# First chunk's attention of a fused attention and two-MLP kernel: two pairs of units with their own buffers in a hand-set order, and W1, W2 decoded 1024 wide

## The chip, the cores and the metric

The kernel runs on one core of one Trainium2 chip. The metric is the device time of one execution in microseconds. Three runs of the kernel before took 773.91, 776.0 and 777.68 us, median 776.0.

## The reference

Three stages follow each other on 4 sequences of 576 positions, model width 512 (8 heads of 64):

```python
# 1. attention, per head: two softmaxes, added
q_d, k_d, v_d = (mean of 4 neighbouring positions of q, k, v)     # 144 rows
out_up = repeat(softmax(scale * q_d @ k_d.T) @ v_d, 4)
out_local = softmax(where(|i - j| < 4, scale * q @ k.T, -1e9)) @ v
x = out_up + out_local                                            # -> (4, 576, 512)
# 2. first MLP, a residual around it
xn = (x - mean(x)) / sqrt(var(x) + 1e-6) * g_ln
x = x + relu(xn @ w_ch1) @ w_ch2                                  # 512 -> 2048 -> 512
# 3. second MLP with a shift by one position
xk = mu_k * x + (1 - mu_k) * x_prev;  xr = mu_r * x + (1 - mu_r) * x_prev
out = sigmoid(xr @ w_r) * (relu(xk @ w_k) ** 2 @ w_v)             # 512 -> 1024 -> 512
```

The weights come in float64. The activations are float32.

## The kernel before

The 2304 positions are cut into six chunks of 384 (`N`). A chunk's attention is four *units*, one per pair of heads (`unit(c, hp, nxt)`). A unit sums q over four positions (line 354, `prep`), sums k (line 357 in chunk 0, by accumulating DMAs later), makes the dense scores of the summed rows (`scd`, line 419) and the windowed scores in 32-column tiles (`sc`, line 423), does the two softmaxes on DVE and ACT (lines 429 to 463), turns the probabilities around (line 477 on DVE for the windowed ones, line 493 on PE for the dense ones, copies at 481 and 496), multiplies by v (`av`, lines 506 and 515) and adds both into `x` (line 524). [...] The first MLP takes its 16 blocks of 128 hidden features in turn (`emit_l1`, `emit_l2`): twelve products (four k-blocks, three products each: high by high, high by low, low by high) give one block of the first layer in `h_ps`, and twelve more add it into the four output banks `acc`.

W1 and W2 arrive as float64, are decoded to float32 and split in two on the chip, piece by piece (`conv_gen`, `decode`). A piece is 128 rows by 512 numbers. It takes three steps on ACT (line 84: the high word, scaled; line 89: the three bits below; line 93: the rounded high part) and three on DVE (line 85: the sign; line 90: shift and or; line 96: the remainder, the low part). The generator does half a piece at each call, and overlaps the last steps of one piece with the first steps of the next. `pieces_w12` gives the order: four pieces of W1, three of W2, and so on, so that a block of W1 comes just ahead of the hidden features that need it. `ensure(key)` runs the generator until a piece is finished; it stands ahead of the products that read the piece.

The order of work is laid down in two ways. The instructions carry dependencies, and a scheduler orders each engine's queue by program order and readiness; `in_order(True, ins)` pins an instruction behind everything that was written for its engine before. In the program text, small generators are advanced in turns: the opening (lines 768 on) issues the first loads in the order of the string `ORDER`, then feeds one `Attn` object with a budget of `PROB` = 800 per turn; it opens a unit when the one before has reached its softmax, so that units overlap by about half; from the tenth turn on the weight generator is called in three of ten turns. When the attention of chunk 0 is over, the first MLP of chunk 0 starts, and `slot(c)` between its products feeds chunk 1's attention and calls the weight generator once (line 803 on). The pinned fillers `idle` (line 375, eight products of 128 columns ahead of each product step) and `warm` (line 365, 512 columns) do no useful work.

Chunk 0's value sums are additions on POOL (lines 345, 346). All loads go out on SP's queue; the accumulating sums for later chunks go out on POOL's queue (lines 324, 325).

Of the kernel before, what the change touches and what calls it, by code (L numbers as in the profile page):

```python
# [8 lines left out]
F32 = mybir.dt.float32  # L9
# [12 lines left out]
SD = S // 4  # L22
# [16 lines left out]
def tile_block(ctx: ExitStack, tc: tile.TileContext, qw, kw, kf, kr, vw, vr, vec, mask, w1, w2, wk, wv, wr, out):  # L39
# [16 lines left out]
    ident = const.tile([2 * QB, 2 * QB], F32, name="ident")  # L56
# [50 lines left out]
    def pieces_w12():  # L107
        for p in range(4):
            yield from (("w1", p, k) for k in range(KT))
            yield from (("w2", f // 4, f % 4) for f in range(max(4 * p - 1, 0), 4 * p + 3 if p < 3 else NF))  # L110

    def conv_gen():
        keys = list(pieces_w12())
        late_keys = [k for k in keys if k[:2] == ("w2", 3)]
        raws, todo = {}, iter([k for k in keys if k not in late_keys])

        def fetch():
            key = next(todo, None)
            while key in raws:
                key = next(todo, None)  # L120
            if key is None:
                return
            nm, p, k = key
            src = w1s[:, :, 1024 * p:1024 * p + 1024] if nm == "w1" else w2s[:, 4 * p:4 * p + 4, :]
            t = wpool.tile([128, 2, 1024], I32, tag="w", name="raw")
            for i in range(2):
                raws[nm, p, k + i] = t[:, i]
            for i in range(2):
                in_order(len(raws) < 9, nc.sync.dma_start(t[:, i], src[:, k + i]))

        def fetch_late(key):
            if key in late_keys:
                t = stg.tile([128, 1024], I32, tag="stg", name="raw", bufs=RB)
                nc.sync.dma_start(t, w2s[:, 12 + key[2], :])
                raws[key] = t
# [7 lines left out]
        for n, key in enumerate(keys + [None]):  # L143
# [3 lines left out]
            if key:  # L147
                nm, p, k = key
# [4 lines left out]
                w1st = next(g)  # L153
# [3 lines left out]
            if last:  # L157
                in_order(pin, split_lo(h, l, w))
                done.add(last)
            if key:  # L160
                h, l, w = W[p][0][:, k, :], W[p][1][:, k, :], w1st
            last = key
            if n % 2 == 1 or n > 24 or n == 4:
                fetch()
# [123 lines left out]
    qds, chains, firsts, raw_k, means = {}, [], [], {}, {}  # L288
# [5 lines left out]
    Ps = [pone.tile([128, 2 * NG, 32], F32, name=f"P{i}") for i in range(2)]  # L294
# [38 lines left out]
    def first_k(hp):  # L333

        if not firsts:
            firsts.append(pln.tile([128, KT, N], F32, tag="xc", name="kf").rearrange("p k n -> p (k n)"))
        t = firsts[0][:, S * (hp % 2):S * (hp % 2) + S]
        in_order(True, nc.sync.dma_start(t, kf[0, hp]))
        kd, _ = sum_tiles(0, hp)
        raw_k[hp] = kd, t  # L340

    def first_v(hp):
        t = xp.tile([128, KT, N], F32, tag=("ah", "al")[hp % 2], name="vr", bufs=1).rearrange("p k n -> p (k n)")[0:KD, 0:1024].rearrange("p (r t d) -> p r t d", r=4, t=2)
        in_order(True, nc.sync.dma_start(t, vr[0, hp].rearrange("r p t d -> p r t d")))
        nc.gpsimd.tensor_tensor(t[:, 0:2], t[:, 0:2], t[:, 2:4], op=ALU.add)
        nc.gpsimd.tensor_tensor(vdt[0, hp], t[:, 0], t[:, 1], op=ALU.add)

    def prep(c, hp):
# [3 lines left out]
        for h in range(2):  # L352
            p = slice(64 * h, 64 * h + 64)
            in_order(c < 2, nc.vector.tensor_reduce(qd[p, :, h, :].rearrange("p i (g t) -> p i g t", g=2), q[p, :, 0:96].rearrange("p (i g) (t r) -> p i g t r", g=2, r=4), axis=AX.X, op=ALU.add))
        if c == 0 and hp in raw_k:
            kd, t = raw_k.pop(hp)
            in_order(True, nc.vector.tensor_reduce(kd, t.rearrange("p (t r) -> p t r", r=4), axis=AX.X, op=ALU.add))
        qds[c, hp] = qd

    def warm(n):  # L360

        ps = ps_acc.tile([128, 512], F32, tag="acc3", name="warm")
        w = W1[0][0]
        for _ in range(n):
            in_order(True, nc.tensor.matmul(ps, w[:, 0, 0:128], w[:, 0, :], start=True, stop=True))
# [3 lines left out]
    def keep_warm(c):  # L369

        if c == 0:
            if not idle_bank:
                idle_bank.append(ps_h.tile([128, 512], F32, tag="h", name="idle"))
            for i in range(8):
                in_order(True, nc.tensor.matmul(idle_bank[0][:, 0:128], ones_r, ones_r, start=True, stop=True))

    def mean_of(c, hp):
        if hp == 0:
            means[c] = ps_h.tile([128, 512], F32, tag="h", name="mean")
        nc.tensor.matmul(means[c][:, 0:N], ones_r.bitcast(F32), xt[c][:, hp, :], start=hp == 0, stop=hp == NHP - 1)  # L380

    def unit(c, hp, nxt):
# [3 lines left out]
        new = c == 0 or runs(c)[1] != runs(c - 1)[1]  # L386
# [15 lines left out]
        if c > 0:  # L402
            while av_user:
                yield GAP
            av_user.append(hp)
            scd = ps_at.tile([128, 512], F32, tag="av", name="scd")
        else:
            scd = ps_acc.tile([128, 512], F32, tag=f"acc{hp}", name="scd")
# [7 lines left out]
        if hp > 0:  # L416
            keep_warm(c)
# [16 lines left out]
        if c == 0 and nxt in loaded:  # L434
            prep(*nxt)
# [760 lines left out]
```

## Time and profile before

| | us |
|---|---|
| median of three runs | 776.0 |
| the profiled execution | 775.27 |
| its span, first to last instruction | 773.2 |
| PE busy | 747.2 (97%) |
| DVE busy | 464.3 (60%) |
| ACT busy | 392.1 (51%) |
| POOL busy | 111.2 (14%) |

The span is what the profile times, and some 2 us of the execution lie around it. PE's busy share is an average over the whole span: in the page's row of 40 slices it is below nine tenths in the first three slices (19.3 us each) and at the end. DVE is at nine tenths and more in the second to fifth slice, and lower from then on. A line number is that of the kernel before; `x` with a number is a count of instructions. A float32 product is two instructions, and the filler and the products of the MLPs, in TensorE's rounded format, are one each.

### The profile page before, as it was taken

What the parts mean: (1) busy time and instruction counts of PE and PEld (TensorE: products, weight loads), DVE (VectorE), ACT (ScalarE), POOL (GpSimd) and SP (SyncE); (2) the same over time, 40 slices, a digit from 0 to 9 for tenths busy, and PEclk for the clock granted to TensorE, in tenths of its full rate; (3) what the DMA queues carried; (4) which work ended last, traced back from release to release, by engine and by line L of the source; (5) the groups of instructions that cost most, each with busy time, mean ns of one, the idle gap of its engine ahead of it and who ended that gap; (6) DMA issues with size and microseconds to landing.
All of it is one profiled execution on the core that took longest, in us unless ns stands there. A gap on an engine that the chain in (4) does not pass through costs nothing.

```text
span 773.2 us, 13981 instructions
## 1 busy us (share of the span) xinstructions
PE 747.2 (97%) x5402; PEld 721.6 (93%) x5402; DVE 464.3 (60%) x909; ACT 392.1 (51%) x832; POOL 111.2 (14%) x144
## 2 busy tenths in 40 slices
PE   5879999999999999999999999999999999999998
PEld 4769899989999989999999999999999999999998
DVE  5879997866556555656576545544898454242311
ACT  3679987454444344445545633334988667421100
POOL 2224310410044401540020003002000000000000
PEclk9979999999999999999999999999999999999999
DMA  8798855365536762774344224913935528686311
GB/s 228 233 301 231 230 141 166 105 196 170 166 115 166 184 173 86 197 174 134 103 158 127 81 80 170 354 70 101 316 136 171 186 100 312 214 281 197 123 62 51
DMA packets 76946, 131.25 MB, mean 170 GB/s; under 512 B 8592, under 2 KB 53776, under 8 KB 75216
## 3 DMA queue, kind: packets, MB, share of 16 engines
q1 hardware_dynamic: 66960, 121.12, 47.7%
q0 software_dynamic: 9920, 9.25, 6.7%
q8 instruction: 42, 0.69, 0.4%
q14 instruction: 24, 0.20, 0.1%
HBM read 89.96 MB, written 40.37 MB: 169 GB/s over the span
## 4 chain that ended last, share of the span: by engine, by line
PE 58%; issue 21%; DMA 10%; DVE 6%; POOL 3%; ACT 3%; SPq 0%; POOLq 0%; DVEq 0%; ACTq 0%
PE b_ps L990 11%; PE b_ps L283 6%; PE b_ps L282 6%; PE b_ps L281 6%; DMA kd<-in_kr 5%; PE acc L282 4%; PE acc L281 4%; PE acc L283 4%; PE h_ps L281 4%; PE h_ps L282 4%; PE h_ps L283 4%; DMA q<-in_qw 1%; POOL x L724 1%; ACT PT L481 1%; PE sc L423 1%
## 5 line engine op out<-in xcount | busy, mean ns | idle before, releaser
L701 ACT ACTIVATE hh<-h_ps 128x384 fp32r<-128x384 f32 x96 | 46.8, 487 | 88.7 <-PE h_ps L283 88.5
L702 DVE SCALAR_TENSOR_TENSOR hl<-h_ps,hh 128x384 fp32r<-128x384 f32 x96 | 53.1, 553 | 58.1 <-ACT hh L701 57.8
L990 PE MATMUL b_ps<-xk,wk 128*128 128x384 f32 x504 | 87.9, 334 | 0.0
L990 PEld LDWEIGHTS b_ps<-xk,wk 128*128 128x128 f32 x504 | 87.5, 188 | 0.0
L724 POOL TENSOR_TENSOR x<-x2t,x 128x384 f32<-128x384 f32 x24 | 24.1, 1023 | 302.3 <-DVE x2t L723 302.1
L281 PE MATMUL b_ps<-ko,wv 128*128 128x384 f32 x192 | 64.1, 334 | 0.0
L282 PE MATMUL b_ps<-ko,wv 128*128 128x384 f32 x192 | 64.1, 334 | 0.0
L283 PE MATMUL b_ps<-ko,wv 128*128 128x384 f32 x192 | 64.1, 334 | 0.0
L1116 DVE TENSOR_TENSOR rin<-b_ps,rin 128x384 f32<-128x384 f32 x24 | 13.4, 557 | 61.1 <-PE b_ps L283 60.6
L481 ACT COPY PT<-T 32x192 f32<-32x192 f32 x96 | 33.5, 349 | 24.6 <-DVE T L477 23.7
L90 DVE SCALAR_TENSOR_TENSOR rm<-rm 128x512 uint32<-128x512 uint32 x52 | 35.8, 691 | 14.7 <-ACT rm L89 14.0
L324 POOL DMA_DIRECT2D kd<-in_kr x36 | 35.4, 983 | 61.6 <-DMA kd<-in_kr 58.9
L325 POOL DMA_DIRECT2D vd<-in_vr x36 | 40.1, 1114 | 24.2 <-DMA vd<-in_vr 20.6
L89 ACT ACTIVATE rm<-raw 128x512 uint8<-128x512 uint8 x52 | 40.3, 786 | 2.2 <-DVE rm L85 2.0
L433 ACT ACTIVATE Pd<-scd,mx 96x144 f32<-96x144 f32 x48 | 17.7, 371 | 38.8 <-DVE mx L430 35.7
L1042 ACT CAST ko<-kin 128x1536 fp32r<-128x1536 f32 x12 | 17.6, 1476 | 38.9 <-PE b_ps L282 22.2
L282 PEld LDWEIGHTS b_ps<-ko,wv 128*128 128x128 f32 x192 | 36.0, 188 | 0.0
L283 PEld LDWEIGHTS b_ps<-ko,wv 128*128 128x128 f32 x192 | 36.0, 188 | 0.0
L281 PEld LDWEIGHTS b_ps<-ko,wv 128*128 128x128 f32 x192 | 36.0, 188 | 0.0
L84 ACT ACTIVATE rm<-raw 128x512 f32<-128x512 f32 x52 | 34.4, 667 | 2.7 <-DMA raw<-in_w 2.3
L1044 DVE TENSOR_TENSOR ko<-kin,ko 128x1536 fp32r<-128x1536 f32 x12 | 20.9, 1754 | 23.4 <-ACT ko L1042 23.3
L281 PE MATMUL h_ps<-ah,w_2h 128*128 128x384 f32 x96 | 33.6, 350 | 0.0
(174 smaller groups left out, 2177.7 us busy)
## 6 DMA issues: line engine op xcount, KB each, us to landing
raw<-in_w SPq DMA_DIRECT2D x32, 512.0 KB, 7.4
kd<-k SPq DMA_DIRECT2D x48, 192.0 KB, 2.8
kin<-kd SPq DMA_DIRECT2D x12, 768.0 KB, 6.1
wk<-wkd SPq DMA_DIRECT2D x7, 1024.0 KB, 7.7
v<-in_vw SPq DMA_DIRECT2D x24, 256.0 KB, 3.4
q<-in_qw SPq DMA_DIRECT2D x24, 208.0 KB, 3.3
kz<-in_kw SPq DMA_DIRECT2D x48, 102.0 KB, 3.7
rd<-r SPq DMA_DIRECT2D x24, 192.0 KB, 1.9
```

What stands on the lines that cost most here:

```text
L84: in_order(pinned, nc.scalar.activation(ru.bitcast(F32), raw.rearrange("p (n t) -> p n t", t=2)[:, :, 1].bitcast(F32), AF.Copy, scale=2.0 ...
L89: in_order(pinned, nc.scalar.activation(low, top, AF.Copy, scale=1.0 / 32.0, bias=-31.0 / 64.0))
L90: in_order(pinned, nc.vector.scalar_tensor_tensor(ru, ru, 3, m, op0=ALU.logical_shift_left, op1=ALU.bitwise_or))
L281: nc.tensor.matmul(ps, wh, ah, start=first, stop=False)
L282: nc.tensor.matmul(ps, wh, al, start=False, stop=False)
L283: nc.tensor.matmul(ps, wl, ah, start=False, stop=last)
L324: in_order(r > 0, eng.dma_start(kd, kr[b, hp, r], **op))
L325: in_order(r > 0, eng.dma_start(vd, vr[b, hp, r], **op))
L481: nc.scalar.copy(PT[p, :, j, :], T[p, :, 0:24])
L701: nc.scalar.activation(hh, ps[:, 0:N], AF.Relu)
L702: last_hl[0] = nc.vector.scalar_tensor_tensor(hl, ps[:, 0:N], 0.0, hh.bitcast(F32), op0=ALU.max, op1=ALU.subtract)
L990: nc.tensor.matmul(ps, a, m[:, k, :], start=start and k + i == 0, stop=k == nk - 1 and i == 2, skip_group_check=True)
```

## The change

- The first chunk's four units become two pairs. A pair does each step for both of its units, most of them with one instruction of twice the length. Each pair has buffers of its own, cut out of slots of the weight pool (`block`), and its own output banks.
- The order of the steps is a string, `FIRST`: `0` and `1` advance a pair by a step, `a` and `b` do a pair's value sums, `w` advances the weight generator. All of these instructions are pinned.
- q is summed over 128 partitions in one instruction for a pair, and the dense scores are taken as 64 x 64 tiles, one per head, in place of a 128-row product with zeros in the other head's half.
- The value sums are on DVE. k's loads and two small ones go out on ACT's queue.
- The fillers are 16 products of 128 columns ahead of everything, eight behind each product step of a pair, and eight of 512 columns behind the last mean.
- W1 and W2 are decoded in pieces of 2 x 512 numbers, W1's and W2's last quarter in pieces of 512. Three pieces are pinned, where six smaller ones were. The generator is called at every other slot of chunk 0, and at every slot from the 37th on. The working tile of a wide piece is a slot of the weight pool.
- The loads and k, v sums for chunk 1's first two units are issued together at the end of the opening.

```diff
-            rm = stg.tile([128, 2, 512], U32, tag="stg", name="rm", bufs=RB)
+            n = raw.shape[1] // 2
+            if n > 512:
+                rm = wpool.tile([128, 2, n], U32, tag="w", name="rm")
+            else:
+                rm = stg.tile([128, 2, n], U32, tag="stg", name="rm", bufs=RB)
...
     def pieces_w12():
-        for p in range(4):
-            yield from (("w1", p, k) for k in range(KT))
-            yield from (("w2", f // 4, f % 4) for f in range(max(4 * p - 1, 0), 4 * p + 3 if p < 3 else NF))
+        for p in range(3):
+            yield from ((nm, p, k, 2) for nm in ("w1", "w2") for k in (0, 2))
+        yield from ((nm, 3, k, 1) for nm in ("w1", "w2") for k in range(4))
...
-            if n % 2 == 1 or n > 24 or n == 4:
+            if key and (key[3] == 2 or key[2] % 2):
                 fetch()
...
+    def load_pair(pr):
+        b = sets[pr]
+        for i in range(2):
+            hp = 2 * pr + i
+            in_order(True, nc.sync.dma_start(b["q"][:, i], qw[hp, :, 0:NG]))
+            for h in range(2):
+                p = slice(64 * h, 64 * h + 64)
+                in_order(True, nc.sync.dma_start(b["kz"][i][p, h], kw[hp, p, 0:NG]))
+            in_order(True, nc.scalar.dma_start(b["kf"][:, i], kf[0, hp]))
...
+    def value_sums(pr):
+        t = vr_01[pr][0:KD]
+        in_order(True, nc.vector.tensor_tensor(t[:, :, 0:2], t[:, :, 0:2], t[:, :, 2:4], op=ALU.add))
+        for i in range(2):
+            in_order(True, nc.vector.tensor_tensor(vdt[0, 2 * pr + i].rearrange("p t d -> p (t d)"), t[:, i, 0], t[:, i, 1], op=ALU.add))
...
+    def pair(pr):
...
+        fixed(nc.vector.tensor_reduce(
+            qd[:, :, :, 0:QB].rearrange("p i j (g t) -> p (i j) g t", g=2),
+            q[:, :, :, 0:96].rearrange("p i (j g) (t r) -> p (i j) g t r", g=2, r=4), axis=AX.X, op=ALU.add))
+        for i in both:
+            fixed(nc.vector.tensor_reduce(kds[0, 2 * pr + i], ...))
+        yield                                  # step 1
...
+                    fixed(nc.tensor.matmul(scd[i][p, j, :], qd[p, i, j, :], kds[0, 2 * pr + i][p, :], start=True, stop=True, tile_position=(64 * h, 64 * h)))
...                                            # windowed scores of both units
+        warm(8)
+        yield                                  # step 2
...                                            # maxima, exponentials: 3; sums, reciprocals, scaling: 4
+        fixed(nc.vector.transpose(T, P))
...                                            # Pd scaled, PT copied, dense ones transposed on PE, PdT copied
+        warm(8)
+        yield                                  # step 5
...                                            # av of both units
+        warm(8)
+        yield                                  # step 6
...                                            # x of both units, each with its mean product
+            mean_of(0, 2 * pr + i)
+        yield                                  # step 7
...
+    warm(EARLY)
+    steps = {"0": pair(0), "1": pair(1), "w": conv}
+    for o in FIRST:
         if o in "ab":
+            value_sums("ab".index(o))
         else:
+            next(steps[o], None)
+    for i in range(2):
+        load_qk(*units[NHP + i])
+    for _ in zip(*[sums(*units[NHP + i]) for i in range(2)]):
+        pass
+    load_v(*units[NHP])
+    warm(WARM, W1[0][0][:, 0, :], 512)
+    for _ in norm(0):
+        pass
...
-        if c == 0:
+        if c == 0 and (slots[c] % 2 or slots[c] > 36):
             next(conv, None)
...
-PINNED = 6
+PINNED = 3
...
-ORDER = "ambcwd"
+ORDER = "w"
+FIRST = "000" "11" "00" "a" "1" "b" "0" "1" "w" "0" "1" "w" "11" "w"
+EARLY = 16
+WARM = 8
```

## Rows read from the trace of the kernel before

**Rows 1.** Busy us by stretch: engine busy (count), PEclk granted clock, DMA share, GB/s.
```profile
0.00:9.00 9.00, 2.23 (x36) 1.67 (x36) 3.48 (x9) 1.46 (x2) 3.16 (x16) 1.00 0.67 186
...
0.00:57.00 57.00, 41.93 (x365) 34.57 (x365) 40.47 (x91) 32.87 (x80) 16.23 (x29) 0.91 0.85 253
...
57.00:113.00 56.00, 54.46 (x472) 51.67 (x473) 53.94 (x121) 51.99 (x112) 16.91 (x19) 1.00 0.76 208
...
45.00:46.00 1.00, 1.00 (x2) 0.51 (x3) 0.93 (x5) 0.58 (x2) 0.19 (x1) 0.50 0.98 291
```

**Rows 2.** The chain of waits around the end of the opening: start, us, what.
```profile
53.85 1.09 PE mean L380 x2
...
57.83 0.45 PE h_ps L282
...
61.94 0.17 PE acc L281
```

**Rows 3.** Timeline of PE in the opening: start, us, engine, line, operation, out<-in, count.
```profile
6.76 1.27 PE L419 MATMUL scd<-kd,qdz 128*96 128x144 f32 x4 [6.76 <-DVE kd L357]
...
19.33 1.55 PE L506 MATMUL av<-PT,v 128*64 128x96 f32 x16
...
21.45 1.97 PE L375 MATMUL idle<-ones_r 128*128 128x128 f32 x8
...
26.73 1.22 PE L419 MATMUL scd<-kd,qdz 128*96 128x144 f32 x4
...
27.88 1.03 PE L423 MATMUL sc<-kz,q 128*32 128x60 f32 x32
...
28.84 1.65 PE L380 MATMUL mean<-x,ones_r 128*128 128x384 f32 x2
...
34.48 0.91 PE L380 MATMUL mean<-x,ones_r 128*128 128x384 f32 x2 [0.81 <-DVE x L524]
...
37.29 0.68 PE L419 MATMUL scd<-kd,qdz 128*96 128x144 f32 x4
...
38.45 1.11 PE L375 MATMUL idle<-ones_r 128*128 128x128 f32 x8
...
39.49 0.88 PE L506 MATMUL av<-PT,v 128*64 128x96 f32 x16
...
40.63 1.11 PE L375 MATMUL idle<-ones_r 128*128 128x128 f32 x8
```

**Rows 4.** Groups by line and shape, 0 to 57.5 us: count | busy us, mean ns.
```profile
L354 DVE TENSOR_REDUCE qdz<-q 64x96 f32<-64x384 f32 x10 | 5.4, 542 | 1.3 <-DMA q<-in_qw 1.2
...
L357 DVE TENSOR_REDUCE kd<-kf 128x144 f32<-128x576 f32 x4 | 3.0, 751 | 1.7 <-DMA kf<-in_kf 1.6
...
L431 DVE TENSOR_TENSOR P<-sc,mask_t 128x240 f32<-128x240 f32 x4 | 1.6, 401 | 0.7 <-PE sc L423 0.7
```

**Rows 5.** Timeline of POOL and DVE at 13 us.
```profile
13.16 1.27 POOL L345 TENSOR_TENSOR vr<-vr 72x512 f32<-72x512 f32 x1 [9.34 <-DMA vr<-in_vr]
...
13.30 1.39 DVE L463 TENSOR_TENSOR P<-P,mx 128x240 f32<-128x240 f32 x1
```

**Rows 6.** Groups by line and shape, 57 to 113 us, then one of the page.
```profile
L84 ACT ACTIVATE rm<-raw 128x512 f32<-128x512 f32 x19 | 12.4, 671 | 0.2
...
L85 DVE TENSOR_SCALAR rm<-rm 128x512 uint32<-128x512 uint32 x19 | 7.8, 423 | 0.2 <-ACT rm L84 0.2
...
L89 ACT ACTIVATE rm<-raw 128x512 uint8<-128x512 uint8 x19 | 14.3, 785 | 0.0
...
L90 DVE SCALAR_TENSOR_TENSOR rm<-rm 128x512 uint32<-128x512 uint32 x19 | 12.9, 685 | 1.2 <-ACT rm L89 1.2
...
L96 DVE TENSOR_TENSOR w_1l<-rm,w_1h 128x512 fp32r<-128x512 f32 x8 | 5.4, 688 | 0.3
...
L1044 DVE TENSOR_TENSOR ko<-kin,ko 128x1536 fp32r<-128x1536 f32 x12 | 20.9, 1754 | 23.4 <-ACT ko L1042 23.3
```

**Rows 7.** Busy us of line 96 (DVE) alone until the second layer starts.
```profile
0.00:61.90 61.90, 5.92 (x8) 0.92 0.87 262
```

More of the change, by code (lines that the diff above doesn't have):

```diff
@@ L152, in conv_gen @@
                 g = decode(raws[key], pin)
-                w1st = next(g)
+                w_next = next(g)
             yield
@@ L158, in conv_gen @@
                 in_order(pin, split_lo(h, l, w))
-                done.add(last)
+                done.update((last[0], last[1], last[2] + i) for i in range(last[3]))
             if key:
-                h, l, w = W[p][0][:, k, :], W[p][1][:, k, :], w1st
+                h, l = (t[:, k:k + m, :].rearrange("p k n -> p (k n)") for t in W[p])
+                w = w_next
             last = key
-            if n % 2 == 1 or n > 24 or n == 4:
+            if key and (key[3] == 2 or key[2] % 2):
                 fetch()
@@ L287, in tile_block @@
     loaded, kds, vdt, vts = {}, {}, {}, {}
-    qds, chains, firsts, raw_k, means = {}, [], [], {}, {}
+    units = [(c, hp) for c in range(NCH) for hp in range(NHP)]
+    qds, chains, means = {}, [], {}
     xt, xsum, stage = {}, {}, {}
@@ L353, in prep, with warm @@
             p = slice(64 * h, 64 * h + 64)
[L354 to L357, printed above, removed]
+            in_order(True, nc.vector.tensor_reduce(qd[p, :, h, :].rearrange("p i (g t) -> p i g t", g=2), q[p, :, 0:96].rearrange("p (i g) (t r) -> p i g t r", g=2, r=4), axis=AX.X, op=ALU.add))
         qds[c, hp] = qd
-    def warm(n):
-        ps = ps_acc.tile([128, 512], F32, tag="acc3", name="warm")
-        w = W1[0][0]
+    idle_bank = []
+    def warm(n, w=None, cols=128):
+        w = ones_r if w is None else w
         for _ in range(n):
-            in_order(True, nc.tensor.matmul(ps, w[:, 0, 0:128], w[:, 0, :], start=True, stop=True))
-    idle_bank = []
-    def keep_warm(c):
-        if c == 0:
[L372 to L375, printed above, removed]
+            in_order(True, nc.tensor.matmul(idle_bank[0][:, 0:cols], w[:, 0:128], w[:, 0:cols], start=True, stop=True))
     def mean_of(c, hp):
@@ L385, in unit @@
         tick()
-        new = c == 0 or runs(c)[1] != runs(c - 1)[1]
+        new = runs(c)[1] != runs(c - 1)[1]
         q, k = loaded.pop((c, hp))
@@ L401, in unit @@
         yield GAP
[L402 to L408, printed above, removed]
+        while av_user:
+            yield GAP
+        av_user.append(hp)
+        scd = ps_at.tile([128, 512], F32, tag="av", name="scd")
         sc = ps_at.tile([128, 512], F32, tag="sc", name="sc")
@@ L464, in unit @@
         yield 340
-        while c + hp > 0 and units[units.index((c, hp)) - 1] not in multiplied:
+        while units[units.index((c, hp)) - 1] not in multiplied:
             yield GAP
@@ L542, in unit @@
             yield 460
-    units = [(c, hp) for c in range(NCH) for hp in range(NHP)]
     rstd, ahi, alo = {}, {}, {}
@@ L754, in tile_block, with block @@
     conv, pre = conv_gen(), pre_b()
+    def block(*parts):
+        t = wpool.tile([128, 2048], F32, tag="w", name="first")
+        n, views = 0, []
+        for m in parts:
+            views.append(t[:, n:n + m])
+            n += m
+        return views
+    QW, KW, KF, PW, TW, PTW, PDW, TDW, VW, QDW = 4 * 104, 2 * NG * (72 + WIN), S, 4 * NG * 32, 4 * NG * 32, 4 * NG * 96, 4 * SD, 8 * 2 * QB, NG * 2 * D, 4 * 64
+    q_0, kf_0 = block(2 * QW, 2 * KF)
+    q_1, kf_1 = block(2 * QW, 2 * KF)
+    kz_1, qd_0 = block(2 * KW, QDW)
@@ new lines, in tile_block @@
+    nc.scalar.dma_start(mask_t, mask)
+    load_pair(0)
+    for hp in range(NHP):
+        sum_tiles(0, hp)
+    for h in range(2):
+        p = slice(64 * h, 64 * h + 64)
+        for i in range(2):
+            nc.vector.memset(kz[i][p, 1 - h], 0.0)
+            nc.gpsimd.memset(sets[1]["kz"][i][p, 1 - h], 0.0)
+    for b in sets:
+        nc.vector.memset(b["qd"][:, :, :, QB:64], 0.0)
+        nc.gpsimd.memset(b["P"], 0.0)
+        nc.gpsimd.memset(b["P"][:, :, WIN:WIN + 1], 1e-9)
+    one = stg.tile([128, 128], F32, tag="stg", name="one", bufs=RB)
```

222 lines of the change are left out of this document (145 added, 77 removed).

## The prediction

> **What bounds the kernel now.** I read the busy table by stretch first. From 57 us on PE is busy nearly all the time (54.5 of 56.0 us in the stretch 57 to 113), and what follows is not touched by the change; in the first 57 us PE is busy 41.9 us, of which much is the filler product `idle`, and nothing of the two large layers is done there [rows 1]. So the span is this opening plus a product stream that nothing here shortens, and the change is worth what it moves the start of that stream. The chain of waits marks the two points I measure by: the last `mean` product of chunk 0 ends at 54.94 us (53.85 + 1.09), and the first product of the second layer (`acc`) stands at 61.94 us [rows 2]. The same table shows the second thing that matters: in 57 to 113 us DVE is busy 53.9 and ACT 52.0 of 56 us [rows 1]. They decode weights there, just ahead of PE. Work that is pushed out of the opening lands on them.
>
> **Part 1, the inputs.** Pair 0 needs q 2 x 208 KB, kz 4 x 102 KB, kf 2 x 288 KB and the mask's 120 KB: 1,520 KB. In the first 9 us the transfers ran at 186 GB/s, 1.67 MB [rows 1]. With pair 1's loads mixed in behind, I put the last input of pair 0 at 9.0 us and its scores at 9.5 (before, one unit's scores started at 6.76 [rows 3]). The kf loads move to ACT's queue. The Trainium skill (DMA: Bandwidth & Descriptors, "Issuing engines are not separate DMA queues") says that loads from different engines still share the same transfer engines, so only issue time is saved; if instead ACT's queue were a channel of its own, kf would be in by about 6 us and the whole opening 1.5 us shorter. No row of this case has a load on ACT's queue.
>
> **Part 2, the reductions and the value sums.** q's sum was two 64-partition reductions of 0.54 us per unit; over 128 partitions for two units it is one of twice that length, bounds 0.54 and 1.08, I take 0.95. Saved over four units: 8 x 0.54 - 2 x 0.95 = 2.4 us of DVE [rows 4]. The value sums leave POOL for DVE: three additions per pair, about 1.1 + 2 x 0.4 us, so +3.8 us on DVE. Against that, POOL's addition at 13.16 us lies beside a 240-wide DVE product that took 1.39 us, where others took 0.40 [rows 4, 5]; four such collisions would be some 4 us. Together near nothing, and DVE is not the longest chain below.
>
> **Part 3, the pair chain.** Pair 0: scores 9.5 to 13.7, then minimum, maximum and subtraction over both units, about 0.65 us each (half the length takes 0.40 [rows 4]), to 15.7; pair 1's reductions (0.95 + 2 x 0.75 [rows 4]) follow on DVE, so PE starts pair 1's scores at about 18. From there PE's written order runs almost without a gap, since the other pair's DVE and ACT work lies beside it. Its length hangs on TensorE's level. At 1.2 GHz one unit costs, from the start of its first product to that of what follows, scores 2.11 us (26.73 to 28.84) and `av` 2.12 (19.33 to 21.45), eight fillers 1.97 and a `mean` 1.65; at 2.4 GHz the same are 1.16 (37.29 to 38.45), 1.14 (39.49 to 40.63), 1.11 and 0.91 [rows 3]. The last two overlap what follows a little: 1.9, 1.6 and 1.04, 0.85. PE's list from pair 1's scores on, for both pairs: scores 4.2, filler 1.9, transposes 1.9 (estimate, eight of 128 columns in place of 96), filler 1.9, `av` 4.2, filler 1.9, `mean` 3.2, transposes 1.9, filler 1.9, `av` 4.2, filler 1.9, `mean` 3.2: 34.3 us at the low level, 18.0 at the high one. So the last `mean` ends at 52 us if PE is slow throughout, and at 36 if it is fast throughout; at the fast end PE no longer covers the DVE and ACT steps, which add about 2.5.
>
> Which level holds is the largest unknown. Before, the filler `idle` took 1.97 us at 21.45 and 1.11 at 38.45 [rows 3]: PE ran at the low level through some ten busy microseconds of filler, scores and `av`, and reached the high one just after the first `mean`, a long full-width product. Later it fell back for a while (granted clock 0.50 in 45 to 46 us [rows 1]). (The granted clock reads 1.00 before that, which the durations deny; I go by the durations.) After the change two units' scores stand back to back, 4.2 us in place of 2.1, and two units' `av` likewise, so PE is loaded in longer stretches; the fillers are the same short product that did not lift the clock before. I take the rise inside pair 0's `av`, near 30 us: 12.0 us of the list are done, 22.3 remain, x 18.0 / 34.3 = 11.7, + 1 of waits: the last `mean` ends at 42.7, 12.2 us earlier than before.
>
> The dense-score products change shape: 64 x 64 tiles in diagonal pairs, eight products per pair of units where there were four. The row of the windowed scores shows four column tiles at once (32 passes of 60 columns in 1.03 us, 32 ns each, against 0.31 us for a pass of 144 [rows 3]); row tiles stand nowhere. The Trainium skill (TensorEngine Tiling (Array Packing), "Key Properties") has different tiles load and multiply in parallel, but says that a change of tiling mode drains the engine. I count them as two at once, no dearer than before; one after the other they would add 2 x 2.4 us at the low level.
>
> **Part 4, what is given back behind the mean.** Before, from the last `mean` to the second layer took 61.94 - 54.94 = 7.0 us. By then eight 512-wide pieces of W1, W2 were finished [rows 7]. The new order finishes none by the mean: behind it DVE must still do the `or` (line 90) of the second 1024-wide piece, the `subtract` (line 96) of the first, the mask (line 85) and `or` of the third and the `subtract` of the second (the steps are pinned behind the four `xc` subtractions). A 1024-wide step, from 512 at 0.69 and 1536 at 1.75 us (`subtract` [rows 6]), is 1.22, or 1.14 with overlap: 4 x 1.14 + 0.6 = 5.2 us, of which before had 0.4. This lies on the path, because the first layer needs all of W1's first block. PE can take some products of the next tile meanwhile, so 7.0 + 5.0 = 12.0; bounds 9 (half hidden) and 13.5 (all serial with ACT's steps between). The second layer starts at 42.7 + 12.0 = 54.7, a gain of 7.2 us.
>
> **Part 5, chunk 0.** Decoding one 512 piece costs DVE 0.42 + 0.69 + 0.69 and ACT 0.67 + 0.79 and a cast [rows 6]. Doubling the width saves only the fixed part, some 0.07 us of a DVE step from start to start and 0.1 of an ACT one: over ten wide pairs 2 us of DVE, 3 of ACT. But the kernel enters the second layer about two pieces behind (6 against 8 subtractions, 3 us of DVE), and a pair counts as ready only when the next pair's first steps are out. With DVE at 96% this costs PE -1 to 4 us; I take 1.2. Chunk 1's sums and loads go out together at the end of the opening, on POOL's and SP's queues, where nothing of chunk 0 waits behind them but raw weights already two pieces ahead; nothing counted. Later chunks are unchanged.
>
> **Sum.** 7.2 - 1.2 = 6.0 us off the profiled execution's 775.27 (773.2 span and 2.1 around it): 769.3. The median of the three runs is 0.7 above that execution; I say 769.6.
>
> **Rivals.**
> - *PE stays at the low level until the means.* For it: ten busy microseconds of the same products did not lift it before. Against: scores and `av` now stand in doubled stretches. Rise at 36 us: 18 of the list done, 16.3 x 0.525 = 8.6, mean end 45.6 with waits, second layer 57.6, gain 4.3 - 1.2: 772.5.
> - *It rises in the first scores.* Mean end 36 + 2.5 + 1 = 39.5, second layer 51.5, gain 10.4, chunk 0 even: about 765.
> - *Slower: the decode falls behind in chunk 0.* The 1024-wide steps are forced out before the second layer and at the three later block borders of W1; each time DVE owes PE one wide pair, 2.9 us. Four borders are 11.5 us, against a gain of 7.2: +4.3, about 780. For it: DVE 96% and ACT 93% busy. Against: those same rows held PE back by only 1.5 us. It decides once PE waits more than 7 us on `w_` tiles in chunk 0.
> - *The pairs don't overlap* (the hand-set order makes PE wait on ACT's copies at each change of pair, about 2 us six times): 12.2 becomes 0, 780 too.
>
> **How the numbers follow.** A difference under 0.5% (3.9 us) can't be told from none here. Forecast 0.45 (its own range 765 to 772), low clock 0.2 (no change that can be told), early clock 0.2 (faster), slower rivals 0.15 in all, a fifth of it within 0.5%. Faster 0.63 (0.43 of the forecast's, and the early clock), same 0.25, slower 0.12. The range 760.5 to 777.5 takes in the early clock with a cheap tail and a quarter of the slower cases.
>
> **What would show it.** Pair 1's scores on PE near 18 us; filler eights at 1.1 us from about 30; the last `mean` at 42.7; five wide DVE steps between it and the last first-layer products; first `acc` at 54.7; waits of PE on weight tiles under 2 us in chunk 0. It is wrong if the opening's PE list has gaps over 3 us in all, or the second layer starts after 60.

## The result, and the profile after

The changed kernel takes 769.25 us, the median of 15 runs (fourteen of 765.74 to 773.82 us; one of 1455.43, in the slow state, is left out of the ratio), against 776.14 for the kernel before beside it: ratio 0.991, 95% interval 0.989 to 0.993. The profiled execution took 768.59 us (before 775.27), its span 766.8 (before 773.2). The forecast was 769.6.

The busy table by stretch, as in [rows 1]:

```profile
0.00:9.00 9.00, 3.68 (x16) 3.49 (x16) 3.56 (x10) 1.58 (x2) 7.29 (x21) 1.00 0.80 232
0.00:57.00 57.00, 40.25 (x383) 34.22 (x384) 37.80 (x68) 31.35 (x63) 18.85 (x35) 0.88 0.96 268
0.00:49.00 49.00, 33.20 (x355) 27.98 (x356) 30.39 (x58) 24.26 (x55) 14.20 (x29) 0.89 0.99 280
```

PE is no busier in the opening than before (40.3 against 41.9 us): the gain isn't that it does more, but that its products of the large layers begin sooner. What is new is in the last row: in the first 49 us the transfers run at a share of 0.99, where the first 57 us before had 0.85 [rows 1] (over the same 57 us it is 0.96 now).

PE's timeline through the opening (start, us, what, and in brackets the idle time ahead and what ended it), to set beside [rows 2, 3]:

```profile
9.03 2.19 PE L826 MATMUL scd<-kd,first 64*64 64x144 f32 x16 [1.91 <-DVE kd L817]
...
16.71 2.18 PE L826 MATMUL scd<-kd,first 64*64 64x144 f32 x16 [1.84 <-DVE kd L817]
...
21.92 1.04 PE L872 MATMUL tp<-ident,first 128*72 128x128 f32 x8
22.71 1.09 PE L354 MATMUL idle<-ones_r 128*128 128x128 f32 x8
23.73 0.88 PE L883 MATMUL av<-first 128*64 128x96 f32 x16
...
32.67 2.93 PE L359 MATMUL mean<-x,ones_r 128*128 128x384 f32 x4 [5.69 <-DVE x L901]
35.39 1.91 PE L872 MATMUL tp<-ident,first 128*72 128x128 f32 x8
...
41.79 1.50 PE L359 MATMUL mean<-x,ones_r 128*128 128x384 f32 x4
...
48.68 0.67 PE L286 MATMUL h_ps<-al,w_0h 128*128 128x384 f32 x1 [2.17 <-DVE al L544]
...
53.91 0.44 PE L287 MATMUL h_ps<-ah,w_0l 128*128 128x384 f32 x1 [0.95 <-DVE w_0l L100]
...
55.46 0.79 PE L285 MATMUL acc<-hh,w_0h 128*128 128x384 f32 x3
```

The first product of the second layer in the same view of the kernel before:

```profile
61.78 0.33 PE L281 MATMUL acc<-hh,w_0h 128*128 128x384 f32 x1
```

The last `mean` (the product with a matrix of 1/512 whose result `norm` subtracts) ends at 41.79 + 1.50 = 43.29 us (before 54.94), the second layer begins at 55.46 (before 61.78; the chain in [rows 2] puts the same product at 61.94): 6.3 us of the span's 6.4. Two things in PE's timeline the forecast did not have. Eight transposes take 1.04 us at 21.92 and 1.91 at 35.39, eight fillers 1.09 at 22.71: by these durations PE reaches the high level near 21.5 us and is at the low one at 35. And between the two it stands for 5.69 us, waiting for pair 0's `x`. The granted clock (the figure before the last two of each row; before 21.5 us it reads 1.00 too, which the durations deny, as they did before the change) places the fall within that idle time, the next rise near 38.5, and a second fall behind the 2.17 us wait, by 49:

```profile
27.00:28.00 1.00, 0.00 (x0) 0.00 (x0) 0.29 (x1) 0.82 (x2) 0.00 (x0) 1.00 0.91 295
28.00:29.00 1.00, 0.00 (x0) 0.00 (x0) 0.97 (x2) 0.00 (x0) 0.00 (x0) 0.63 0.78 282
38.00:39.00 1.00, 1.00 (x11) 0.93 (x12) 0.00 (x0) 1.00 (x1) 1.00 (x3) 0.75 1.18 288
49.00:50.00 1.00, 1.00 (x4) 1.00 (x4) 0.78 (x3) 1.00 (x2) 0.29 (x1) 0.50 1.09 331
```

DVE's timeline says what `x` waited for (the first and the last three rows serve the points further down), and the chain of waits in the second fence says where that began:

```profile
7.36 0.95 DVE L813 TENSOR_REDUCE first<-first 128x192 f32<-128x768 f32 x1 [4.30 <-DMA first<-in_qw]
...
27.71 1.22 DVE L768 TENSOR_TENSOR first<-first 72x1024 f32<-72x1024 f32 x1 [3.11 <-DMA first<-in_vr]
28.96 0.76 DVE L770 TENSOR_TENSOR vd<-first 72x256 f32<-72x256 f32 x2
29.64 0.66 DVE L854 TENSOR_REDUCE sm<-first 128x16 f32<-128x496 f32 x1
...
32.06 0.55 DVE L901 TENSOR_TENSOR x<-av,ud 128x384 f32<-128x384 f32 x1
...
45.74 1.22 DVE L94 SCALAR_TENSOR_TENSOR rm<-rm 128x1024 uint32<-128x1024 uint32 x1
46.88 1.22 DVE L100 TENSOR_TENSOR w_0l<-rm,w_0h 128x1024 fp32r<-128x1024 f32 x1
48.01 1.14 DVE L544 SCALAR_TENSOR_TENSOR al<-xc,vec_t,ah 128x384 fp32r<-128x384 f32 x2
```

```profile
16.03 11.59 DMA first<-in_vr
27.71 1.23 DVE first L768
```

Pair 1's raw values (288 KB a unit) were issued by 16.0 us and landed at 27.6. DVE's queue is in the written order, where `b`, the sum over those values, stands ahead of pair 1's softmax sums and pair 0's `x`. So DVE stood 3.11 us with pair 0's `av` finished, and PE stood behind it.

### The profile page after: what moved, and what is told of

Same layout as the page of the kernel before. It is cut to its first block, busy times and chain, and to the rows that moved or that the text cites. A ratio compares the mean times of both kernels' runs of the same rounds, so it can differ in the third digit from the quotient of the medians.

```text
span 766.8 us, 13866 instructions
## 1 busy us (share of the span) xinstructions
PE 740.9 (97%) x5390; PEld 716.0 (93%) x5390; DVE 455.3 (59%) x856; ACT 386.8 (50%) x786; POOL 107.5 (14%) x141
## 4 chain that ended last, share of the span: by engine, by line
PE 50%; issue 26%; DMA 13%; POOL 5%; DVE 4%; ACT 2%; SPq 0%; POOLq 0%; ACTq 0%; DVEq 0%
PE b_ps L1127 11%; PE b_ps L286 7%; PE b_ps L285 7%; PE b_ps L287 7%; DMA kd<-in_kr 5%; DMA vd<-in_vr 3%; PE acc L286 3%; PE acc L285 3%; PE acc L287 3%; PE h_ps L285 3%; PE h_ps L286 3%; PE h_ps L287 3%; POOL x L681 2%; DMA first<-in_vr 2%; POOL vd L331 1%
## 5 line engine op out<-in xcount | busy, mean ns | idle before, releaser
L94 DVE SCALAR_TENSOR_TENSOR rm<-rm 128x512 uint32<-128x512 uint32 (+1 forms) x40 | 33.8, 846 | 14.7 <-ACT rm L93 14.2
L93 ACT ACTIVATE rm<-raw 128x512 uint8<-128x512 uint8 (+1 forms) x40 | 38.5, 965 | 3.6 <-DVE rm L89 3.1
L1179 ACT CAST ko<-kin 128x1536 fp32r<-128x1536 f32 x12 | 17.6, 1476 | 38.9 <-PE b_ps L286 23.1
L88 ACT ACTIVATE rm<-raw 128x512 f32<-128x512 f32 (+1 forms) x40 | 32.3, 809 | 5.3 <-DMA raw<-in_w 4.4
L286 PE MATMUL h_ps<-al,w_0h 128*128 128x384 f32 x96 | 32.7, 345 | 2.2 <-DVE al L544 2.2
L1181 DVE TENSOR_TENSOR ko<-kin,ko 128x1536 fp32r<-128x1536 f32 x12 | 20.9, 1754 | 22.8 <-ACT ko L1179 22.7
L286 PE MATMUL acc<-hl,w_0h 128*128 128x384 f32 x96 | 32.8, 342 | 1.0 <-DVE hl L659 0.7
L285 PE MATMUL h_ps<-ah,w_0h 128*128 128x384 f32 x96 | 32.8, 344 | 0.8 <-ACT ah L543 0.8
```

The lines of the kernel that those rows point to most:

```text
L88: in_order(pinned, nc.scalar.activation(ru.bitcast(F32), raw.rearrange("p (n t) -> p n t", t=2)[:, :, 1].bitcast(F32), AF.Copy, scale=2.0 ...
L93: in_order(pinned, nc.scalar.activation(low, top, AF.Copy, scale=1.0 / 32.0, bias=-31.0 / 64.0))
L94: in_order(pinned, nc.vector.scalar_tensor_tensor(ru, ru, 3, m, op0=ALU.logical_shift_left, op1=ALU.bitwise_or))
L285: nc.tensor.matmul(ps, wh, ah, start=first, stop=False)
L286: nc.tensor.matmul(ps, wh, al, start=False, stop=False)
```

## The experiments

Each was run beside the kernel before on the same chip. The change itself has 0.991 (0.989 to 0.993); a ratio's interval is some 0.002 to 0.003 to either side.

**The wait for the raw values, three ways.** First, `b` moved behind pair 0's `x`:

```
-FIRST = "000" "11" "00" "a" "1" "b" "0" "1" "w" "0" "1" "w" "11" "w"
+FIRST = "000" "11" "00" "a" "1" "0" "1" "w" "0" "b" "1" "w" "11" "w"
```

> Only the letter b in FIRST moves: pair 1's value sums are put behind pair 0's x instead of ahead of pair 0's softmax sums. Theory (the wait for pair 1's raw values sets the opening): in the changed kernel DVE stands 3.1 us for that load with pair 0's sums, x and mean queued behind it, PE idles 5.7 us and falls to its low level. Then here pair 0's x comes near 27.5 us in place of 32.1, the mean products of pair 0 start near 28.5 in place of 32.7, the second layer starts 4 to 6 us earlier (50 to 51.5 in place of 55.5): about 764 us. Rival (the chain through pair 1's own steps and the weight decode is as late anyway): the wait moves to the new place of b, the second layer stays within 1.5 us of 55.5: 768 to 770 us.

Measured 767.2 us, ratio 0.9885 (0.9864 to 0.9906): 2 us, less than expected, and the interval overlaps that of the change. PE's timeline:

```profile
12.83 1.11 PE L354 MATMUL idle<-ones_r 128*128 128x128 f32 x8
...
25.73 1.55 PE L883 MATMUL av<-first 128*64 128x96 f32 x16
...
30.66 1.50 PE L359 MATMUL mean<-x,ones_r 128*128 128x384 f32 x4
...
35.97 1.15 PE L883 MATMUL av<-first 128*64 128x96 f32 x16 [2.08 <-issue]
...
40.66 1.50 PE L359 MATMUL mean<-x,ones_r 128*128 128x384 f32 x4
```

The wait is gone. But in this execution the level rose early, at about 12.5 us (eight fillers take 1.11 us at 12.83), fell again while PE waited 2.71 us ahead of pair 1's scores, and was back only at about 29.5 (pair 0's `av` at 25.73 takes 1.55 us, not 0.88). And the sums now hold up pair 1's block transpose on DVE (32.51 to 33.2 us), for which PE waits 2.08 us ahead of `av`. The `mean` gains 1.1 us of the 5.7.

Second, pair 1's values loaded ahead of the first raw weights:

```
-    next(conv)
     load_pair_v(1)
     load_pair_vr(1)
+    next(conv)
```

> The first raw weight piece (1 MB) is issued behind pair 1's v and raw values instead of ahead of them; nothing else. Theory (the same wait, and it is a matter of bytes ahead in the queue): 1 MB less ahead at 280 GB/s lets the raw values land 3.5 us earlier, at about 24 us, DVE's 3.1 us of waiting goes, PE's idle stretch shrinks from 5.7 to about 2.5 us, the second layer starts 3 us earlier or more if TensorE keeps its high level: 764 to 766.5 us. Rival (weights then arrive late instead): the first decode step waits on its load by up to 3.5 us and holds ACT and DVE; the second layer is within 1 us of 55.5: 768 to 770 us.

Measured 767.64 us, ratio 0.9881 (0.986 to 0.9902), again overlapping the change. DVE waits 0.95 us for the values in place of 3.11, PE 0.70 in place of 5.69, the last `mean` ends at 40.77, the second layer begins at 53.37:

```profile
26.22 1.22 DVE L768 TENSOR_TENSOR first<-first 72x1024 f32<-72x1024 f32 x1 [0.95 <-DMA first<-in_vr]
```

```profile
31.24 1.83 PE L359 MATMUL mean<-x,ones_r 128*128 128x384 f32 x4 [0.70 <-DVE x L901]
...
53.37 0.96 PE L285 MATMUL acc<-hh,w_0h 128*128 128x384 f32 x4
```

The first edit leaves the load where it was and frees the other pair's chain; the second moves the load alone and shortens the wait itself. So the wait came from the load's place in a full queue of transfers, and its price from the place of `b`. That time is gained is clear of noise only in the best version below. Third, the value sums on POOL, where the kernel before had them:

```
-        in_order(True, nc.vector.tensor_tensor(...))    # three in value_sums
+        in_order(True, nc.gpsimd.tensor_tensor(...))
```

> Only the value sums go back from DVE to POOL. Theory (DVE's wait for pair 1's raw values delays pair 0's x; collisions between POOL's additions and DVE cost about 1 us each): DVE no longer stands for the load, pair 0's x comes near 28 us, three or four DVE steps are stretched by about 1 us; the two nearly cancel, 767 to 769.5 us. Rival (the collisions weigh more than the wait, as they did before the change): 770 us or more.

Measured 770.47 us, ratio 0.9914 (0.9885 to 0.9944): no change. DVE is free of the wait, but POOL needs 2.36 us for the step that takes DVE 1.22, and behind pair 0's sums in its queue stands the clearing of the `PT` buffers (line 797). ACT waits for that 4.69 us ahead of its copies into `PT`, and PE 4.71 us ahead of `av`. Another queue that works in order took the wait over. And beside POOL's additions DVE is slower again: a step of 0.17 us takes 1.97 at 20.43. POOL, DVE, ACT and PE:

```profile
20.00 2.36 POOL L768 TENSOR_TENSOR first<-first 72x1024 f32<-72x1024 f32 x1 [14.46 <-DMA first<-in_vr]
```

```profile
20.43 1.97 DVE L844 TENSOR_SCALAR mx<-mx 128x4 f32<-128x4 f32 x1
```

```profile
25.21 2.07 ACT L867 COPY first<-first 32x384 f32<-32x384 f32 x4 [4.69 <-POOL first L797]
```

```profile
27.88 1.55 PE L883 MATMUL av<-first 128*64 128x96 f32 x16 [4.71 <-issue]
```

**The order by hand.** Pair 0 to its end, then pair 1; buffers, widths and sums as changed:

```
+FIRST = "000" "00" "a" "0" "w" "0" "111" "w" "11" "b" "1" "w" "1"
```

> Pair 0's attention is issued to its end before pair 1's begins (decoding steps at the same places by their count); buffers, widths and sums as in the changed kernel. Theory (the saving before the mean comes from pair 1's scores and softmax lying beside pair 0's): the last mean ends 4 to 8 us later than 43.3, at 47 to 51, the second layer at 59 to 63, and the time is 4 to 7 us longer, 773 to 776, ratio 0.996 to 1.000. Rival (the work of each pair on VectorE and ScalarE adds up in either order, so that the order gives little): the last mean within 2 us of 43.3, ratio 0.990 to 0.994.

Measured 777.98 us, ratio 1.0009 (0.9984 to 1.0034). All of the gain is gone, somewhat more than the overlap was expected to be worth; the last `mean` ends at 51.71, the second layer begins at 64.00. While one pair's softmax runs on DVE and ACT, PE has nothing:

```profile
18.82 1.92 PE L872 MATMUL tp<-ident,first 128*72 128x128 f32 x8 [4.01 <-ACT first L864]
...
42.43 2.02 PE L872 MATMUL tp<-ident,first 128*72 128x128 f32 x8 [8.12 <-ACT first L864]
...
50.21 1.50 PE L359 MATMUL mean<-x,ones_r 128*128 128x384 f32 x4
```

```profile
38.79 1.23 DVE L94 SCALAR_TENSOR_TENSOR rm<-rm 128x1024 uint32<-128x1024 uint32 x1 [3.35 <-ACT rm L93]
39.93 0.66 DVE L854 TENSOR_REDUCE sm<-first 128x16 f32<-128x496 f32 x1
```

Of the 8.12 us, 3.35 are this order's own: its second `w` puts a decoding step that waits for ACT ahead of pair 1's softmax sums. Without that it might have kept some 3 us; that was not run. Its ten runs also have a lower mean granted clock (0.982, the changed kernel's fourteen 0.990), so part of the price may be the level's.

**The width.** Pieces of 512 again, twice the `w`s, so that as many columns are decoded at the same places:

```
-        for p in range(3):
-            yield from ((nm, p, k, 2) for nm in ("w1", "w2") for k in (0, 2))
-        yield from ((nm, 3, k, 1) for nm in ("w1", "w2") for k in range(4))
+        for p in range(4):
+            yield from ((nm, p, k, 1) for nm in ("w1", "w2") for k in range(4))
-PINNED = 3
+PINNED = 6
```

> Only the width of decode is undone: all of W1 and W2 in pieces of 512, six pinned, two generator steps where the changed kernel has one, every slot of chunk 0 calling it. Theory (the width saves only the fixed part of each step, 2 to 3 us of DVE and ACT in chunk 0, which PE hardly waits for, and gives it back by coarser steps): within 1.5 us of the changed kernel, 768 to 771 us. Rival (the width is what keeps chunk 0 from falling behind): PE waits in chunk 0 grow by 3 us or more, 772 us and above.

Measured 773.96 us, ratio 0.9958 (0.9937 to 0.998). The width is worth about half of the gain, 3.7 us; I had it near nothing. The last `mean` ends at 45.35 us, 2.1 later, the second layer begins 3.0 later, and the rest (below) takes 713.8 us in place of 711.3, with some 7 us at the low level. How much of this is the steps' fixed part and how much their finer mixture with the softmax, and how much the level's in this one execution, isn't told apart by this run.

**The tail behind the mean.** Two decoding steps in a fixed order instead of three:

```
-PINNED = 3
+PINNED = 2
```

> PINNED 2 in place of 3: the decode steps of the third wide piece (W2's first) are no longer held ahead of the remainder of the second piece. Theory (what is given back behind the mean is decode on DVE and ACT ahead of the last first-layer products): mask and or of the third piece, 0.6 + 1.14 us of DVE with 1.15 + 1.37 of ACT in the chain between them, leave the path; the first layer's last products come 1.5 to 3 us earlier, the second layer starts near 53: 766 to 768 us. Rival (the tail is bound by the second piece's own steps, or the third piece is then late for the second layer by as much): no change within 1 us, 768 to 770.

Measured 773.23 us, ratio 0.9955 (0.9936 to 0.9974), the wrong way. Let go, the scheduler puts the low part of the second piece and the `or` of the third ahead of the last three `al` (the low parts of the first layer's input), and the second layer begins at 57.56 us. DVE:

```profile
49.18 0.61 DVE L544 SCALAR_TENSOR_TENSOR al<-xc,vec_t,ah 128x384 fp32r<-128x384 f32 x1
49.71 1.22 DVE L100 TENSOR_TENSOR w_0l<-rm,w_0h 128x1024 fp32r<-128x1024 f32 x1
50.85 1.22 DVE L94 SCALAR_TENSOR_TENSOR rm<-rm 128x1024 uint32<-128x1024 uint32 x1
51.98 1.67 DVE L544 SCALAR_TENSOR_TENSOR al<-xc,vec_t,ah 128x384 fp32r<-128x384 f32 x3
```

From the last `mean` to the second layer it is 14.5 us in place of 12.2, so the order of DVE's queue does set the tail. Not all of the 4 us lost need be that: the twelve runs have a mean granted clock of 0.983 in place of 0.990. Next, W1's first quarter holds a constant, with none of its copies and subtractions; its loads stay:

```
+        W1[0] = wtiles("w1_0")                  # filled with 0.03 by POOL
+        done.update(("w1", 0, k) for k in range(4))
```

> The first quarter of W1 (two wide pieces) is not decoded; its tiles hold a constant, its loads stay, and the decode steps of the opening go to W2's first pieces. Theory (12.2 us from the last mean to the second layer, 5 more than before, because wide decode steps of W1's first quarter stand on DVE and ACT between them): that stretch falls to 7.5 to 9 us, the second layer starts near 51.5, and chunk 0 has two wide pieces less to decode: 763 to 766 us. Rival (the stretch is long for another reason, such as the level of TensorE or ACT's order): it stays over 11 us, 768 us or more.

Measured 770.83 us, ratio 0.9917 (0.9887 to 0.9946). From the last `mean` (44.24 us) to the second layer (51.98) it takes 7.7 us, as expected, against 12.2: decoding is 4.5 us of the tail. Yet the whole is no shorter. 1.0 us went ahead of the `mean`: the first piece to be decoded is now W2's, whose load stands behind W1's unused ones, and ACT waits 4.97 us for it ahead of DVE's first mask. The rest went here, by PE's timeline and the busy table (line numbers are 5 higher in this kernel):

```profile
71.92 0.44 PE L292 MATMUL h_ps<-ah,w_1l 128*128 128x384 f32 x1 [1.85 <-DVE w_1l L100]
```

```profile
71.00:72.00 1.00, 0.08 (x1) 0.08 (x1) 1.00 (x2) 0.99 (x3) 0.00 (x0) 1.00 1.00 394
72.00:73.00 1.00, 1.00 (x4) 0.66 (x4) 1.00 (x1) 0.95 (x4) 0.79 (x1) 0.71 1.08 332
73.00:74.00 1.00, 1.00 (x13) 0.91 (x14) 0.01 (x1) 1.00 (x2) 0.12 (x1) 0.50 1.09 369
...
159.00:160.00 1.00, 0.07 (x1) 0.00 (x0) 0.00 (x0) 0.00 (x0) 0.00 (x0) 1.00 1.05 399
...
163.00:164.00 1.00, 1.00 (x22) 0.84 (x15) 0.60 (x3) 0.67 (x4) 0.00 (x0) 0.50 0.87 254
```

PE got to W1's second block 1.85 us before its low part, and twice, at 72 and at 161 us, an idle stretch of some 2 us was followed by a spell of 3 to 4 us at the low level. In such a spell products start every 0.32 us and not every 0.17, so it costs about half its length.

**What becomes of an earlier start.** From the second layer's start to the end of the span, by profiled execution, with the time at the low level behind that start (twice the shortfall of the granted clock from 1 times the stretch, good to about 1 us):

```
                     second layer   rest of the span   at the low level
before                    61.78          711.4              0
after                     55.46          711.3              0
POOL sums                 56.04          710.7              0
b behind pair 0's x       54.55          712.0              3
values loaded first       53.37          712.5              3
two steps fixed           57.56          713.1              3
pairs one by one          64.00          713.1              5
no fillers                53.37          713.5              3
wide fillers              55.32          714.3              4
512-wide pieces           58.48          713.8              7
W1's first quarter        51.98          714.7              7
best version (below)      52.91          710.7              0
```

Where PE keeps its level, the rest is 711 us whenever it begins. The 0.7 to 3.4 us that the others give back go with low spells. Why one idle stretch of 2 us is followed by such a spell and another isn't (the changed kernel's PE stands 2.06 us near 103 us and keeps its level; with `b` moved it stands 1.88 us at the same place and loses it) stays open. For chunk 0's pace without them, W2's last quarter was left a constant (not decoded, its loads left out):

```
-        keys = list(pieces_w12())
+        keys = list(pieces_w12())[:-4]          # W2[3] filled with 0.03 by POOL
```

> W2's last quarter is a constant instead of being decoded (all of its loads, copies and subtractions are gone; the products stay). Some 7 us of VectorE and 7 us of ScalarE leave the stretch from 60 to 134 us. Theory (the first chunk gives back an earlier start because decoding on VectorE and ScalarE sets its pace): TensorE's idle time between 55 and 134 us falls from some 5 us to under 2, and the time by 2 to 5 us; 764 to 767, ratio 0.984 to 0.988. Rival (the pace there is TensorE's and the idle time is that of attention's own waits): the idle time stays within 1 us, and the time within 1 us, ratio 0.990 to 0.992.

Measured 767.53 us, ratio 0.9876 (0.9842 to 0.9911); the second layer begins at 55.72, as in the changed kernel, and the rest takes 709.1 us with no low spell. From 55 to 200 us DVE has 5.7 us less to do and ACT 7.4, and that is worth 2 to 3 us (the ratio's interval overlaps that of the change): decoding seems to set a part of that stretch's pace. PE's idle time from 55 to 134 us falls only from 3.2 to 2.5 us, so the first theory fits in its sign and in the time, not in where it put the idle time.

**The fillers.** All fillers of 128 columns left out of the pairs and ahead of them, or made 512 columns wide:

```
-    warm(EARLY)
-        warm(8)            # three per pair
```

> The sixteen early fillers and the eight behind each product step of a pair are left out; the last eight stay. Theory (the opening is long because of TensorE's level, which the dense stretches and fillers lift): without them PE stays at 1.2 GHz up to the means, the transposes, av and means take 1.8 times as long, 3 to 6 us more: 772 to 775 us. Rival (the opening is bound by loads, DVE and ACT, and the fillers only stand in PE's way): no change or 1 us less, 768 to 769.5.

Measured 771.82 us, ratio 0.9929 (0.99 to 0.9957): some 1.5 us slower, within both intervals. Its profiled execution reached the high level at 21 us without them. So it rises without them too.

```
-    warm(EARLY)
-        warm(8)
+    warm(8, None, 512)
+        warm(4, None, 512)
```

> The fillers of 128 columns become fillers of 512 columns: eight ahead of everything in place of sixteen, four behind each product step in place of eight, about the same PE time. Theory (TensorE's level is the largest uncertain term: long full-width products lift it, the short fillers often don't): the level rises in the early fillers and holds through the opening, so pair 1's scores, the transposes, av and means run at the 2.4 GHz durations in every execution; the second layer starts 1.5 to 4 us earlier than with the short fillers (51.5 to 54), and the runs lie closer together than the 8 us of the changed kernel: about 766 us. Rival (level hardly matters, the chain waits for loads, DVE and ACT in the gaps anyway): 768 to 770, and the same spread.

Measured 769.96 us, ratio 0.9907 (0.988 to 0.9934): no change. The level rose at about 15, fell at 18.3, and rose and fell twice more by 49; PE still waited 4.95 us for `x`. A filler can't cover a wait that is several times its length.

**The best version.** The three runs on the wait point to one place for `b`, behind pair 1's block transpose and ahead of its `av`, where DVE had 5 us to spare:

```
+FIRST = "000" "11" "00" "a" "1" "0" "1" "w" "0" "1" "b" "w" "11" "w"
```

> Pair 1's value sums stand behind pair 1's block transpose on VectorE, so neither pair 0's softmax sums nor pair 1's transpose wait for the raw values. Theory (what was left over when the sums stood behind pair 0's x was the 1.97 us for which they held up pair 1's block transpose): pair 1's transpose near 30.6 us instead of 32.5, the last mean done near 40.5 instead of 42.2, the second layer at 52.5 to 53.5, and 1 to 2.5 us less than with the sums behind pair 0's x; 764.5 to 767, ratio 0.985 to 0.988. Rival (the low level of TensorE's clock takes back what a wait gives): no more than 0.7 us less than there, ratio 0.988 or above.

Measured 765.26 us (764.36 to 766.56), ratio 0.9843 (0.9818 to 0.9867), 0.7% below the change as it was made, with no overlap of the intervals. PE:

```profile
30.43 1.50 PE L359 MATMUL mean<-x,ones_r 128*128 128x384 f32 x4
...
33.82 0.88 PE L883 MATMUL av<-first 128*64 128x96 f32 x16 [0.16 <-issue]
...
37.28 1.83 PE L359 MATMUL mean<-x,ones_r 128*128 128x384 f32 x4 [0.22 <-DVE x L901]
...
52.91 0.99 PE L285 MATMUL acc<-hh,w_0h 128*128 128x384 f32 x4
```

No wait before a `mean` is over 0.22 us, the last one ends at 39.11 (4.2 us earlier), and the rest of the span is 710.7 us. The tail takes 13.8, mostly since the first layer's products run at the low level here (0.52 us each at 46.6 to 52.6).

On top of it, the low part of a piece issued ahead of the next piece's second half:

```
-            if key:
-                next(g, None)
             if last:
                 in_order(pin, split_lo(h, l, w))
+            if key:
+                next(g, None)
```

> As the run with the sums behind pair 1's block transpose, and the low part of the piece before (VectorE, 1.22 us) is issued ahead of the second half of the decoding of the next one. Theory (VectorE's queue sets the time from the mean to the second layer): the low part that the last products of the first unit wait for is there 1.2 us earlier, and the second layer starts 0.7 to 1.5 us earlier, 51.3 to 52.5; ratio 0.001 to 0.002 lower. Rival (the scheduler moves other steps in its place, as with two steps in a fixed order): no earlier, and the ratio within 0.001 of it or above.

Measured 767.24 us, ratio 0.9871 (0.9846 to 0.9897): nothing gained. In its profiled execution the tail is shorter, 12.5 us from the `mean` to the second layer at 52.66, and the second low part done 1.2 us earlier, as expected; but the `mean` itself came 1 us later (the level rose early, fell again in a wait of 2.27 us, and pair 1's transposes were slow), and a low spell of 4 us at 161 follows. The edit is right for its place and too small beside the level.

## Why the prediction was right, and where it wasn't

- **The bound** held: what the change moves is the second layer's start, 6.3 us, and the rest of the span is 711.4 us before and 711.3 after. (DVE is at nine tenths in the fourth to sixth slice of the page before, the stretch where chunk 0's weights are decoded, not in the second to fifth.)
- **Parts 1 and 2** held. Pair 0's scores start at 9.03 (9.5 predicted), pair 1's at 16.71 (about 18). The 128-partition sum of q takes 0.95 us as taken, the value sums 1.22 + 0.76 per pair, 4.0 us in all (3.8). Pair 0 waits for q (DVE until 7.36, above); the transfers ran at 232 GB/s in the first 9 us, where 186 was taken. kf, from ACT's queue, is summed at 8.23 without a wait; the scores came 0.5 us early, not the 1.5 of a channel of its own, which is with the rule of the Trainium skill (DMA: Bandwidth & Descriptors, "Issuing engines are not separate DMA queues") and doesn't prove it. The dense scores in 64 x 64 tiles are 16 passes in 2.18 us, 0.14 each against 0.31 for one before [rows 3], so two at once, as the Trainium skill (TensorEngine Tiling (Array Packing), "Key Properties") has it; of its drain at a change of mode no row shows anything.
- **Part 3 came out right by two errors that cancel.** The step "I take the rise inside pair 0's `av`, near 30 us" failed: in the profiled execution the level rose near 21.5 and fell again in the gap; in the others it rose first between 12 and 22, and where that was by 15 it fell again and came back at 20 to 30. And PE's list does not run "almost without a gap": it had one of 5.69 us, more than the 3 us that were named as what would make the prediction wrong. The list was also added up wrongly: its items give 32.3 us at the low level and 17.6 at the high one, not 34.3 and 18.0, and the same step with these ends at 42.1. From 42.7: -1.3 for the earlier start, -3.8 for a list that took 20.9 us of PE in place of 24.7 (0.6 of it that sum), +5.7 for the gap, is 43.3, as measured. What I missed could be read beforehand: in the kernel's text pair 1's raw values are the last of the first chunk's attention loads on SP's queue, behind W1's first raw weights, the sum over them is written ahead of pair 0's `x`, and [rows 1] had the transfers at a share of 0.85 already. The value sums were priced by their duration alone, not by when their data lands.
- **Part 4** held, but for a sum of 4.8 us (5.2 less 0.4) that was taken as 5.0: 12.2 us from mean to second layer (12.0), with the five wide DVE steps named, 1.22 us each (1.22) and 0.69 for the mask.
- **Part 5**: 1.2 us for a decode that is behind was not lost; the rest of the span is even. That too hides in the total: the second layer began 6.3 us earlier, not 7.2, and nothing was given back, which comes to the 6.0 forecast within 0.3. "Doubling the width saves only the fixed part" under-counted it: 512-wide pieces lose half of the gain.
- **The rivals.** "The pairs don't overlap" is what the run one by one does. It was priced at 4 us above the kernel before; measured it can't be told from the kernel before beside it (777.98 against 777.4), so the price was too high by some 3 us. The slow decode did not come (PE waits 1.0 us on `w_0l` after 50 us). The early clock nearly came in the profiled execution (behind pair 1's scores), without its 765, since the wait took it back, and the level with it.

## What to carry to other kernels

When a change writes the order of an in-order queue by hand, write beside each step not only how long it takes but when its input lands: one sum that waited 3.1 us for a load held up the other pair's chain, and PE stood 5.7 us; moving it five letters on in the order gave 0.7%, three quarters of the change's own gain again. When an opening is shortened, compare what is left from a fixed point to the end; if that differs between variants, look for idle stretches of PE and the low level behind them before blaming the new step. A total that fits is no proof of its terms.

## What was not expected of the hardware

- TensorE's level changed five times in the first 56 us of the changed kernel's profiled execution. Its first rise came near 21.5 us there and at about 12.5 with `b` moved, though PE's work is the same up to that place; and the early rise was no gain, since the level fell again by 16 us and was back only at about 29.5.
- The fourteen runs of the changed kernel spread over 8 us, the six of the best version, where PE has no gap over 2.8 us in the opening behind its first product, over 2.2. Over the fourteen the time goes with the mean granted clock of the run (correlation -0.8: 0.984 in the two longest, 772.28 and 773.82 us; 0.992 and 0.996 in the two shortest, 765.74 and 766.96). So the level is bound up with the spread; what makes it differ from run to run is not shown, and six runs spread less than fourteen in any case.
